# Attention with a selective layer: transposes in banks of the scores, and up to three small tasks per opening

## The chip, the cores and the metric

The kernel runs on one core of one Trainium2 chip. The metric is the time on the device in microseconds (us), the median of several runs. The engines are named as the profile names them: PE is TensorE (matmuls and transposes), PEld its weight loads, DVE is VectorE, ACT is ScalarE, POOL is GpSimd, SP is SyncE, which issues transfers.

## What is computed

Attention over 8 batches, 12 heads, 448 tokens and a head size of 64, in fp32; queries and keys are normalised before. The result, heads side by side, is the input x (448 tokens of 768 numbers per batch) of a layer that only 128 tokens of each batch pass through: those with the highest score.

```python
def rmsnorm(x, g):
    rms = np.sqrt(np.mean(x * x, axis=-1, keepdims=True) + 1e-06)
    return x / rms * g
q_n, k_n = (rmsnorm(q, g_q), rmsnorm(k, g_k))
scores = scale * np.matmul(q_n, k_n.transpose(0, 1, 3, 2))
scores = scores - np.max(scores, axis=-1, keepdims=True)
attn = np.exp(scores)
attn = attn / (np.sum(attn, axis=-1, keepdims=True) + 1e-09)
out = np.matmul(attn, v)
# ... heads side by side: x is (B, S, H * D)
scores = np.einsum('bsd,d->bs', x, w_gate)
out = x.copy()
for b in range(B):
    top_idx = np.argpartition(-scores[b], capacity)[:capacity]
    xe = x[b, top_idx]
    h = np.maximum(xe @ w1, 0.0)
    ye = h @ w2
    g = 1.0 / (1.0 + np.exp(-scores[b, top_idx]))
    out[b, top_idx] = x[b, top_idx] + g[:, None] * ye
```

## The kernel before

Four heads make a group; there are 24 groups, three to a batch. A group has 7 units of 64 keys, so 168 units in all. A round q of the main loop takes four units: scores and values in turn, two units at a time, and then openings, in which small tasks and pieces of the layers of an earlier batch are put between.

The kernel divides eight banks of PSUM so: four in a ring for the scores (two for each unit), two for the values, one called aux and one called moe.

```python
ps_sc = ctx.enter_context(tc.tile_pool(name="ps_sc", bufs=4, space=PSUM))
ps_av = ctx.enter_context(tc.tile_pool(name="ps_av", bufs=2, space=PSUM))
ps_aux = ctx.enter_context(tc.tile_pool(name="ps_aux", bufs=1, space=PSUM))
ps_moe = ctx.enter_context(tc.tile_pool(name="ps_moe", bufs=1, space=PSUM))

def aux(shape, name):
    if PER * now[0] >= units:              # attention is over
        return ps_sc.tile(shape, F32, tag="sc", name=name)
    if spare[0]:                           # no piece of the layers here
        return ps_moe.tile(shape, F32, tag="moe", name=name)
    return ps_aux.tile(shape, F32, tag="aux", name=name)
```

When the last unit of a group has its values, four tasks follow. `sum_keys` multiplies the sums of the probabilities with a small matrix (den_ps, line 360), and ACT copies the result to SBUF (den). `invert_sums` transposes it (denT_ps, line 375), and DVE takes the reciprocal (rden). `to_tokens` transposes the result of a pair of heads (x_ps, line 389; two pairs in a group, c = 0 and 1), and DVE multiplies it with rden into x (line 391). `last_tokens` does pair 1 and lets the gate scores follow.

```python
def to_tokens(n, c):
    # ...
    t = xTs.pop((n, c))
    ps = aux([128, NJ, 128], "x_ps")
    for j in range(NJ):
        nc.tensor.transpose(out=ps[:CP, j, :], in_=t[:, j, :], identity=ident)
    # ... DVE: x = ps * rden

def finish(n, q):
    # ...
    task((q, 1), sum_keys, n)
    task((q, 2), invert_sums, n)
    task((q + 1, 0), to_tokens, n, 0)
    task((q + 1, 1), last_tokens, n)
```

An opening does one task, the first that is due. When a batch's x is whole, `score_rows` transposes the gate scores (row_ps, line 444), ACT copies them to SBUF (score_rows), DVE ranks the tokens, and the selected rows go through DRAM and come back as xe. `mixture` is a generator of pieces: two halves of the selected rows' transposes (line 523), the first product (line 542), the second (line 561); its banks are moe's.

```python
for a in range(2):
    ps = bank()                            # ps_moe, or ps_sc after the attention
    for i in range(half):
        nc.tensor.transpose(...)           # 3 x 128 columns of xe
    nc.scalar.copy(out=xeT[...], in_=ps[...])
    # ...
    yield
```

The main loop, where `ready` holds the round from which a batch's layers may start:

```python
def opening(q, place):
    now[:] = q, place
    for i, (when, fn) in enumerate(tasks[:2]):
        if when <= (q, place):
            tasks.pop(i)
            fn()
            return

while done < B or tasks:
    now[:] = q, 0
    k = PER * q
    for half in range(HALVES):
        for u in (k + 2 * half, k + 2 * half + 1):
            if u < units:
                scores(u)                  # two banks of the ring, 8 matmuls, 2 exps on ACT
        run_values(k + 2 * half - 1, q)    # 8 matmuls a unit; DVE sums the probabilities
    opening(q, 0)
    for half in range(HALVES):
        run((k + 2 * half, k + 2 * half + 1))   # loads, squares, scaling, gate ...
        some = piece(q)                    # a piece of the layers, if there is one
        spare[0] = not some and half == 0
        if some or half == 0 or len(tasks) > 2:
            opening(q, half + 1)
        spare[0] = False
        run(())
    q += 1
```

Instructions stand on each engine in the order of the program.

Of the kernel before, what the change touches and what calls it, by code (L numbers as in the profile page):

```python
# [10 lines left out]
F32 = mybir.dt.float32  # L11
# [57 lines left out]
def fast(  # L69
# [23 lines left out]
    B, NP, _, S = loads.src["qT"].shape  # L93
    CP = 112
    NJ = S // CP
# [24 lines left out]
    ps_sc = ctx.enter_context(tc.tile_pool(name="ps_sc", bufs=4, space=PSUM))  # L120
# [4 lines left out]
    spare = [False]  # L125

    def aux(shape, name):

        if PER * now[0] >= units:
            return ps_sc.tile(shape, F32, tag="sc", name=name)  # L130
        if spare[0]:
            return ps_moe.tile(shape, F32, tag="moe", name=name)
        return ps_aux.tile(shape, F32, tag="aux", name=name)

# [23 lines left out]
    ps = ps_moe.tile([128, 512], F32, tag="moe", name="warm_ps")  # L158
# [121 lines left out]
    def scores(u):  # L280
        n, i = divmod(u, NI)
        scs = [ps_sc.tile([128, 512], F32, tag="sc", name="sc") for _ in range(2)]
        for c in range(2):
            for k0 in (0, 32):
                for hh in range(2):
                    r = slice(D * hh, D * (hh + 1))
                    o = D * c + k0
                    nc.tensor.matmul(  # L288
                        out=scs[hh][o : o + 32, 0:S],
                        lhsT=get("kT", n)[r, c, D * i + k0 : D * i + k0 + 32],  # L290
                        rhs=get("qT", n)[r, c, :],
                        start=True,
                        stop=True,
                    )
        p = p_pool.tile([128, 2, S], F32, name="p")
        for hh in range(2):
            nc.scalar.activation(  # L297
                out=p[:, hh],
                in_=scs[hh][:, 0:S],
                func=AF.Exp,  # L300
                scale=rinvs[n, 1][:, hh, i : i + 1],
            )
        probs[u] = p
# [78 lines left out]
    def to_tokens(n, c):  # L382
        b = n // NG
        if b not in xs:
            xs[b] = x_pool.tile([CP, NJ, DX], F32, name="x")
        t = xTs.pop((n, c))
        ps = aux([128, NJ, 128], "x_ps")
        for j in range(NJ):
            nc.tensor.transpose(out=ps[:CP, j, :], in_=t[:, j, :], identity=ident)  # L389
        col = (n % NG * 2 + c) * 128  # L390
        nc.vector.tensor_tensor(  # L391
            out=xs[b][:, :, col : col + 128].rearrange("p j (h d) -> p j h d", d=D),
            in0=ps[:CP].rearrange("p j (h d) -> p j h d", d=D),
            in1=rdens[n][:, :, :, c, None].to_broadcast([CP, NJ, 2, D]),
            op=OP.mult,
        )
# [109 lines left out]
    def mixture(b):  # L506

        n = CAP
        xe = xes.pop(b)
        xeT = moe_pool.tile([128, NDC, 128], F32, name="xeT")  # L510

        def bank():

            if PER * now[0] >= units:
                return ps_sc.tile([128, 512], F32, tag="sc", name="sc")
            return ps_moe.tile([128, 512], F32, tag="moe", name="moe_ps")

        half = NDC // 2
        for a in range(2):
            ps = bank()  # L520
            for i in range(half):
                dc = half * a + i
                nc.tensor.transpose(
                    out=ps[:, 128 * i : 128 * i + n],
                    in_=xe[:n, 128 * dc : 128 * (dc + 1)],
                    identity=ident[:n, :n],
                )
            nc.scalar.copy(
                out=xeT[:, half * a : half * (a + 1), :n],
                in_=ps[:, : half * 128].rearrange("p (i t) -> p i t", t=128)[:, :, :n],  # L530
            )
            if a == 1:
                row = moe_pool.tile([128, 1], I32, name="row", bufs=2)
                nc.vector.tensor_copy(out=row[:n], in_=xe[:n, DM + 1 : DM + 2])
            yield

        hT = moe_pool.tile([128, NFC, 128], F32, name="hT")
        for f0 in range(0, NFC, 4):
            ps = bank()
            for i in range(4):  # L540
                for dc in range(NDC):
                    nc.tensor.matmul(  # L542
                        out=ps[:, 128 * i : 128 * i + n],
                        lhsT=w1[:, dc, 128 * (f0 + i) : 128 * (f0 + i + 1)],
                        rhs=xeT[:, dc, :n],
                        start=(dc == 0),
                        stop=(dc == NDC - 1),
                    )
                if i == 1:
                    yield  # L550
            nc.scalar.activation(
                out=hT[:, f0 : f0 + 4, :n],
                in_=ps.rearrange("p (i t) -> p i t", t=128)[:, :, :n],
                func=AF.Relu,
            )
            yield
        for a in range(2):
            cols = slice(DM // 2 * a, DM // 2 * (a + 1))
            ps = bank()
            for fc in range(NFC):  # L560
                nc.tensor.matmul(  # L561
                    out=ps[:n, : DM // 2],
                    lhsT=hT[:, fc, :n],
                    rhs=w2[:, fc, cols],
                    start=(fc == 0),
                    stop=(fc == NFC - 1),
                )
                if fc == NFC // 2 - 1:
                    yield
            nc.vector.scalar_tensor_tensor(  # L570
                out=xe[:n, cols],
                in0=ps[:n, : DM // 2],
                scalar=xe[:n, DM : DM + 1],
                in1=xe[:n, cols],
                op0=OP.mult,
                op1=OP.add,
            )
            if a == 1:
                nc.gpsimd.indirect_dma_start(  # L579
                    out=out.flatten_outer_dims(),  # L580
                    out_offset=bass.IndirectOffsetOnAxis(ap=row[:n, :1], axis=0),
                    in_=xe[:n, 0:DM],
                    in_offset=None,
                )
            yield
# [9 lines left out]
    todo, tasks = {}, []  # L595
# [4 lines left out]
    now = [0, 0]  # L600

    def task(when, fn, *args):
        tasks.append((when, lambda: fn(*args)))

    def opening(q, place):
        now[:] = q, place
        for i, (when, fn) in enumerate(tasks[:2]):
            if when <= (q, place):
                tasks.pop(i)
                fn()  # L610
                return

    def prepare(n, slot):
        sq = {}
# [23 lines left out]
    def finish(n, q):  # L638

        if n == n_groups - 1:  # L640
            for fn, args in ((sum_keys, (n,)), (invert_sums, (n,)), (to_tokens, (n, 0))):
                task((q, 1), fn, *args)
            task((q, 1), last_tokens, n)
            return
        task((q, 1), sum_keys, n)
        task((q, 2), invert_sums, n)
        task((q + 1, 0), to_tokens, n, 0)
        task((q + 1, 1), last_tokens, n)

    def soon():  # L650

        q, place = now
        return PER * q + 2 * place if PER * q < units else -9
# [30 lines left out]
    def run_values(upto, q):  # L684
        ended = False
        while waiting and waiting[0] <= upto:
            u = waiting[0]
            if ended and u % NI == 0:

                return  # L690
            values(waiting.pop(0))
            if u % NI == NI - 1:
                values_out(u // NI)
                finish(u // NI, q)
                ended = True
            add_probs(u)
# [11 lines left out]
    def run(slots):  # L708
        for slot in sorted(x for x in todo if x < 0 or x in slots):
            for fn in todo.pop(slot):  # L710
                fn()
# [14 lines left out]
    moe, ready, done, q = iter(()), {}, 0, 0  # L726
# [6 lines that stand above are left out]
                    scores(u)  # L733
            run_values(k + 2 * half - 1, q)
        opening(q, 0)
        for half in range(HALVES):
            run((k + 2 * half, k + 2 * half + 1))
            some = piece(q)
            spare[0] = not some and half == 0
            if some or half == 0 or len(tasks) > 2:  # L740
                opening(q, half + 1)
            spare[0] = False
            run(())
        q += 1
# [532 lines left out]
```

## Time and profile before

| what | value |
|---|---|
| time, median of 3 runs | 543.69 us (543.24 to 544.44) |
| span of the profiled run | 541.9 us |
| mean granted clock of PE | 0.993 |
| ACT busy | 278.2 us (51%) |
| POOL busy | 242.3 us (45%) |
| transfers | 93.57 MB, mean 173 GB/s |
| first product of the layers (line 542) begins | 126.9 us |
| last product of the layers ends | 531 us |

A line of a group in the profile gives the source line, the engine, the operation, what it writes and reads, the shape and the count; then the busy time in us and the mean duration of one in ns; then the idle time of the engine just ahead of it, and what ended most of it. A line of the timeline gives start and length in us, and the count of the instructions that it merges; in square brackets, the idle time before it and who ended it. PE has two records for each fp32 matmul, so a unit's 8 score matmuls stand there as 16 records and a pair of units as 32. Matmuls that run side by side in parts of the array overlap in the records; their ends are modelled.

### The profile page before, as it was taken

To read this page: it belongs to the slowest core of one execution; us is meant where nothing else is said; L and a number is where in the kernel's file an instruction comes from. 1 tells how busy PE (TensorE), PEld (TensorE's weight loads), DVE (VectorE), ACT (ScalarE), POOL (GpSimd) and SP (SyncE) were. 2 spreads that over 40 slices of the span, in tenths; PEclk is the share of its full clock that TensorE was granted. 3 is DMA by queue.
4 is the path that set the end of the run, shared out by engine and by line. 5 is a ranking of instruction groups with operands and counts; after the bars stand their busy time and mean duration, and the time that the engine had idled before them with its cause. 6 is when DMAs were issued, how large, how long until landed. Compare 5 with 4: busy or idle time off the path is not lost. (4 is left out here: it accounts for less than half of the span.)

```text
span 541.9 us, 16470 instructions
## 1 busy us (share of the span) xinstructions
PE 514.9 (95%) x7116; PEld 288.7 (53%) x7116; DVE 339.8 (63%) x644; ACT 278.2 (51%) x506; POOL 242.3 (45%) x193
## 2 busy tenths in 40 slices
PE   6999899999999999999999999999999999999991
PEld 5534344446644375546644466443664456568770
DVE  3767898888475776659557794668746384343000
ACT  3787786784535754446445745547454344311000
POOL 4876988558624176244634456246732103002000
PEclk9999999999999999999999999999999999999997
DMA  8857879999951496508726486605924031004100
GB/s 308 340 164 245 283 245 340 300 304 306 299 181 36 145 256 209 199 31 249 223 101 206 137 250 215 206 2 161 288 86 137 31 104 60 2 20 141 60 4 33
DMA packets 41605, 93.57 MB, mean 173 GB/s; under 512 B 6454, under 2 KB 24374, under 8 KB 41524
## 3 DMA queue, kind: packets, MB, share of 16 engines
q1 hardware_dynamic: 36772, 85.96, 50.1%
q0 software_dynamic: 4608, 6.47, 3.6%
q8 instruction: 58, 0.95, 0.7%
q14 instruction: 23, 0.19, 0.1%
q10 hardware_dynamic: 144, 0.00, 0.0%
HBM read 74.93 MB, written 25.35 MB: 185 GB/s over the span
## 5 line engine op out<-in xcount | busy, mean ns | idle before, releaser
L297 ACT ACTIVATE p<-sc,rinv 128x448 f32<-128x448 f32 x336 | 186.3, 639 | 109.7 <-PE sc L288 88.7
L314 PE MATMUL av<-p,v 64*32 64x448 f32 x2688 | 159.2, 537 | 0.0
L288 PE MATMUL sc<-qT,kT 64*32 64x448 f32 x2688 | 153.1, 540 | 0.3
L212 POOL TENSOR_TENSOR rinv<-ss,neg_half 128x14 f32<-128x14 f32 x48 | 138.6, 2888 | 4.0
L331 DVE TENSOR_TENSOR sum<-sum,p 128x896 f32<-128x896 f32 x113 | 122.5, 1084 | 8.9 <-ACT p L297 1.7
L314 PEld LDWEIGHTS av<-p,v 64*32 64x32 f32 x2688 | 58.7, 107 | 78.1 <-issue 72.0
L209 POOL TENSOR_SCALAR ss<-ss 128x14 f32<-128x14 f32 x48 | 22.8, 475 | 160.4 <-DVE ss L208 134.4
L288 PEld LDWEIGHTS sc<-qT,kT 64*32 64x32 f32 x2688 | 49.4, 106 | 70.0 <-issue 47.4
L542 PE MATMUL moe_ps<-xeT,w 128*128 128x128 f32 x576 | 69.4, 277 | 0.8 <-issue 0.8
L208 DVE TENSOR_REDUCE ss<-sq 128x14 f32<-128x896 f32 x48 | 51.4, 1077 | 29.7 <-ACT sq L202 26.1
L542 PEld LDWEIGHTS moe_ps<-xeT,w 128*128 128x128 f32 x576 | 66.3, 192 | 5.1 <-issue 5.1
L391 DVE TENSOR_TENSOR x<-x_ps,rden 112x512 f32<-112x512 f32 x48 | 32.9, 689 | 55.1 <-PE x_ps L389 50.8
L561 PE MATMUL moe_ps<-w,hT 128*128 128x384 f32 x176 | 61.2, 491 | 0.0
L485 POOL DMA_INDIRECT selected<-x,rank x32 | 36.2, 1131 | 35.0 <-DVE x L477 26.2
L202 ACT ACTIVATE sq<-tok 128x896 f32<-128x896 f32 x48 | 45.9, 962 | 6.8 <-DMA tok<-in_tok_dram 6.7
L579 POOL DMA_INDIRECT out_dram<-xe,row x8 | 10.8, 1354 | 79.8 <-DVE rden L377 47.7
L561 PEld LDWEIGHTS moe_ps<-w,hT 128*128 128x128 f32 x176 | 31.7, 190 | 21.8 <-issue 2.9
L415 DVE SCALAR_TENSOR_TENSOR prod<-x,wg 112x256 f32<-112x256 f32 x96 | 40.9, 426 | 3.0
L226 POOL DMA_DIRECT2D rows<-rinv x44 | 29.1, 662 | 6.6 <-POOL rinv L212 6.5
L389 PEld LDWEIGHTS x_ps<-ident,xT 128*112 128x112 f32 x192 | 21.0, 133 | 18.9 <-issue 12.7
L389 PE MATMUL x_ps<-ident,xT 128*112 128x128 f32 x192 | 29.1, 278 | 1.4 <-DVE x L391 1.4
L570 DVE SCALAR_TENSOR_TENSOR xe<-sc,xe 128x384 f32<-128x384 f32 x5 | 3.1, 618 | 41.0 <-PE sc L561 41.0
(66 smaller groups left out, 339.7 us busy)
## 6 DMA issues: line engine op xcount, KB each, us to landing
tok<-in_tok_dram SPq DMA_DIRECT2D x48, 448.0 KB
qT<-in_qT_dram SPq DMA_DIRECT2D x24, 448.0 KB
kT<-in_kT_dram SPq DMA_DIRECT2D x24, 448.0 KB
v<-in_vp_dram SPq DMA_DIRECT2D x24, 448.0 KB
out_dram<-x SPq DMA_DIRECT2D x8, 1344.0 KB
bc<-rows SPq DMA_DIRECT2D x44, 224.0 KB
xe<-selected SPq DMA_DIRECT2D x8, 385.0 KB
w<-in_moe_w_dram SPq DMA_DIRECT2D x6, 512.0 KB
```

The costliest lines, as they stand in the source:

```text
L202: nc.scalar.activation(out=sq, in_=t, func=AF.Square, scale=scale)
L208: nc.vector.tensor_reduce(out=ss, in_=sq, axis=AX.X, op=OP.add)
L212: nc.gpsimd.tensor_tensor(out=rinv.rearrange(flat), in0=ss.rearrange(flat), in1=neg_half.to_broadcast([128, 2 * NI]), op=OP.pow,)
L288: nc.tensor.matmul(out=scs[hh][o : o + 32, 0:S], lhsT=get("kT", n)[r, c, D * i + k0 : D * i + k0 + 32], rhs=get("qT", n)[r, c, :], start=True,
L297: nc.scalar.activation(out=p[:, hh], in_=scs[hh][:, 0:S], func=AF.Exp, scale=rinvs[n, 1][:, hh, i : i + 1],)
L314: nc.tensor.matmul(out=avs[n][c][o : o + 32, 0:S], lhsT=get("v", n)[r, hh, i, d0 : d0 + 32], rhs=probs[u][r, hh], start=(i == 0), stop=(i ...
L331: nc.vector.tensor_tensor(out=sums[n], in0=probs[u - 1] if i == 1 else sums[n], in1=probs[u], op=OP.add)
L389: nc.tensor.transpose(out=ps[:CP, j, :], in_=t[:, j, :], identity=ident)
L415: nc.vector.scalar_tensor_tensor(out=prod, in0=xs[b][:, j, cols], scalar=1.0, in1=wg[:, cols], op0=OP.mult, op1=OP.mult, accum_out=gates[b ...
L485: w = nc.gpsimd.indirect_dma_start(out=t[:, :], out_offset=bass.IndirectOffsetOnAxis(ap=rank[:, j : j + 1], axis=0), in_=x[:, j, :], in_of ...
L542: nc.tensor.matmul(out=ps[:, 128 * i : 128 * i + n], lhsT=w1[:, dc, 128 * (f0 + i) : 128 * (f0 + i + 1)], rhs=xeT[:, dc, :n], start=(dc == 0),
L561: nc.tensor.matmul(out=ps[:n, : DM // 2], lhsT=hT[:, fc, :n], rhs=w2[:, fc, cols], start=(fc == 0), stop=(fc == NFC - 1),)
```

## The change

It does four things. The transposes of pair 1 (c = 1) take a bank of the scores' ring instead of aux. So does the second half of the selected rows' transposes, instead of moe. As long as no layers are ready, an opening does up to three tasks, the inversion and both pairs are due together at the beginning of the next round, and the transposed sums take the moe bank, which nothing else needs yet. In that stage the rule of the spare bank no longer applies to other tasks. The aim is that PE need not wait for the one aux bank and the one moe bank to be read before it goes on.

```diff
@@ -128,7 +128,7 @@
 
         if PER * now[0] >= units:
             return ps_sc.tile(shape, F32, tag="sc", name=name)
-        if spare[0]:
+        if spare[0] or name == "denT_ps" and before_layers(now[0]):
             return ps_moe.tile(shape, F32, tag="moe", name=name)
         return ps_aux.tile(shape, F32, tag="aux", name=name)
 
@@ -384,7 +384,8 @@
         if b not in xs:
             xs[b] = x_pool.tile([CP, NJ, DX], F32, name="x")
         t = xTs.pop((n, c))
-        ps = aux([128, NJ, 128], "x_ps")
+        shape = [128, NJ, 128]
+        ps = ps_sc.tile(shape, F32, tag="sc", name="x_ps") if c else aux(shape, "x_ps")
         for j in range(NJ):
             nc.tensor.transpose(out=ps[:CP, j, :], in_=t[:, j, :], identity=ident)
         col = (n % NG * 2 + c) * 128
@@ -517,7 +518,8 @@
 
         half = NDC // 2
         for a in range(2):
-            ps = bank()
+
+            ps = ps_sc.tile([128, 512], F32, tag="sc", name="xeT_ps") if a else bank()
             for i in range(half):
                 dc = half * a + i
                 nc.tensor.transpose(
@@ -604,11 +606,12 @@
 
     def opening(q, place):
         now[:] = q, place
-        for i, (when, fn) in enumerate(tasks[:2]):
-            if when <= (q, place):
-                tasks.pop(i)
-                fn()
-                return
+        for _ in range(3 if before_layers(q) else 1):
+            for i, (when, fn) in enumerate(tasks[:2]):
+                if when <= (q, place):
+                    tasks.pop(i)
+                    fn()
+                    break
 
     def prepare(n, slot):
         sq = {}
@@ -643,9 +646,18 @@
             task((q, 1), last_tokens, n)
             return
         task((q, 1), sum_keys, n)
+        if before_layers(q):
+
+            task((q + 1, 0), invert_sums, n)
+            task((q + 1, 0), to_tokens, n, 0)
+            task((q + 1, 0), last_tokens, n)
+            return
         task((q, 2), invert_sums, n)
         task((q + 1, 0), to_tokens, n, 0)
         task((q + 1, 1), last_tokens, n)
+
+    def before_layers(q):
+        return done == 0 and ready.get(0, q + 1) > q
 
     def soon():
 
@@ -736,7 +748,7 @@
         for half in range(HALVES):
             run((k + 2 * half, k + 2 * half + 1))
             some = piece(q)
-            spare[0] = not some and half == 0
+            spare[0] = not some and half == 0 and not before_layers(q)
             if some or half == 0 or len(tasks) > 2:
                 opening(q, half + 1)
             spare[0] = False
```

## The prediction

> **What bounds the kernel now.** I read the page's busy times first, then the groups, then the waits of TensorE (PE), then the timelines of PE and VectorE (DVE) around the transposes.
>
> ```profile
> PE 514.9 (95%) x7116; PEld 288.7 (53%) x7116; DVE 339.8 (63%) x644; ACT 278.2 (51%) x506; POOL 242.3 (45%) x193
> L314 PE MATMUL av<-p,v 64*32 64x448 f32 x2688 | 159.2, 537 | 0.0
> L288 PE MATMUL sc<-qT,kT 64*32 64x448 f32 x2688 | 153.1, 540 | 0.3
> ```
>
> PE works almost without a break from 5 us to 531 us, and the idle time in front of its two largest groups is nil, so only waits of PE itself are worth anything. Its waits, longest first, leaving out the start:
>
> ```profile
> PE moe_ps L523 <- ACT xeT L528: 2.1, 3, 1.2
> PE den_ps L360 <- DVE x L391: 2.1, 5, 0.5
> PE denT_ps L375 <- ACT den L368: 1.8, 3, 0.9
> PE denT_ps L375 <- DVE prod L415: 1.4, 1, 1.4
> PE x_ps L389 <- DVE x L391: 1.4, 3, 0.5
> ```
>
> Columns: total us, times, longest. All five are waits for a bank, or for the den copy in SBUF, and sum to 8.8 us: 1.6% of 543.7. That is the ceiling of what the change can take away.
>
> Matmul spans overlap, so I also measure from start to start. In the timeline a block of 32 score or value matmuls (two units) takes 1.50 us (38.24 to 39.74), so a unit 0.75, and the four blocks of a round 6.2 us. Four rounds are 2 to 3 us longer (near 89, 138, 391 and 450 us) where PE's weight loads show only "issue"; I take these as random and keep them.
>
> DVE is at 63% on average, but the table by windows shows 9.69, 9.48 and 9.50 busy us of 10 from 60 to 90 us, the stage before the layers, where the new task rule acts.
>
> **What the Trainium skill says.** "Perfetto Trace Analysis", [...]"Optimizing Tensor Performance", Matmuls: independent groups should rotate through different banks, so that evacuation overlaps the next group. That is the idea of the change; the 8.8 us agree that single banks cost something. "PSUM — Partial Sum Buffer", section "Engine vs sequencer instructions": VectorE and ScalarE queues are strict FIFO and matmuls start in program order. The trace agrees, and this decides my sign: a score matmul that waits for a bank holds everything behind it, and a bank's reader stands behind all earlier work of its engine.
>
> **The change part by part.** The order of instructions in the changed program has as many matmuls in the fast part as before; nothing is computed less.
>
> *Removed.* (a) Before the layers denT moves behind the next round: its four waits go, 1.8 + 1.4 = 3.2 us. (b) Pair 1 no longer waits for the aux bank: 1.4 us. (c) Of the five waits of den for DVE x, three come after pair 1 and go (0.46 + 0.45 + 0.46 = 1.4); two (44 and 103 us) stay, as pair 0 is still in aux. (d) The second half of the selected rows does not wait for the first copy (2.1 us), but denT follows it and needs the den copy, which ACT does behind that same copy: at 311.83 for 0.36 us, so denT could start at about 312.25, against 312.38 now. Worth 0.15 us each, 0.5 in all. (e) Some six fewer switches between small and full array tiles, about 0.1 us each (a block's last gap is 0.09 us longer): 0.6. Sum: 3.2 + 1.4 + 1.4 + 0.5 + 0.6 = 7.1 us.
>
> *Added: pair 1 in the ring of the scores.* The ring has four banks, a unit takes two. Pair 1 takes one; the next unit takes two, and the second bank of the unit after that is pair 1's. Its matmuls start 0.78 us after the first unit's and then wait for DVE to read pair 1. The trace has what that costs:
>
> ```profile
> 51.66 0.60 PE L389 MATMUL x_ps<-ident,xT 128*112 128x128 f32 x4
> 52.19 1.73 PE L288 MATMUL sc<-qT,kT 64*32 64x448 f32 x32
> 50.76 2.29 DVE L331 TENSOR_TENSOR sum<-sum,p 128x896 f32<-128x896 f32 x2
> 52.96 0.25 DVE L377 RECIPROCAL rden<-denT_ps 112x16 f32<-112x16 f32 x1
> 53.32 0.69 DVE L391 TENSOR_TENSOR x<-x_ps,rden 112x512 f32<-112x512 f32 x1
> ```
>
> DVE reads pair 0 here 1.1 us after the scores have begun, because of its sums. With three tasks per opening the order is denT, pair 0, pair 1, scores, and on DVE rden, x, x. Let T be the end of the values. PE reaches the second unit at T + 0.22 + 0.87 + 0.09 + 0.78 = T + 1.96. DVE, if idle, gets pair 0 at T + 0.86 (data lands 0.31 us after the last start) and ends pair 1 near T + 2.25: a wait of 0.3 us. Where DVE is late by its sums, more. Carrying DVE's queue forward op by op with the traced steps (ss 1.0, sum 1.07 to 1.15, gate product 0.47, scaling 1.07, x 0.65):
> - the openings now at 51.7, 67.8, 84.0 and 110.7 us have scores right behind: DVE ends pair 1 near 54.1, 68.9, 86.6 and 112.8 in the changed order, and PE reaches the second unit near 52.6, 68.6, 84.5 and 112.3; waits 1.5, 0.3, 2.1 and 0.5 = 4.4 us
> - at 42.9 and 101.9 us the den matmuls stand between; scores are free, but den's wait for pair 0 grows from 0.35 to 0.5: 0.3 us.
>
> *Added: spare bank not used before the layers.* den now follows row_ps in aux and needs the score_rows copy: near 75 us 0.8 us (copy ends at 76.19 in the trace, and the order of the two is the same); near 118 us row_ps moves a round earlier and the copy stands behind two xT copies (0.98 us), 1.6 us. Together 2.4.
>
> *Added: with layers.* Pair 1 right before scores, no product of the layers between:
>
> ```profile
> 302.96 0.69 DVE L391 TENSOR_TENSOR x<-x_ps,rden 112x512 f32<-112x512 f32 x1 [2.48 <-PE x_ps L389]
> 303.56 1.07 DVE L208 TENSOR_REDUCE ss<-sq 128x14 f32<-128x896 f32 x1
> 304.56 0.68 DVE L391 TENSOR_TENSOR x<-x_ps,rden 112x512 f32<-112x512 f32 x1
> ```
>
> The ss stands between the two reads also in the changed order. Pair 1 is read until 305.24 and the second unit would begin at 303.29 + 0.78 = 304.07: 1.2 us. In the same way 0.6 at 243 us, and 0.15 each at 283, 364 and 386: 2.2 us. Where a product of the layers follows (2.7 us), nothing.
>
> *Added: selected rows in the ring.* Their copy stands on ACT behind a Square of 0.96 us in four of six places:
>
> ```profile
> 181.27 0.50 ACT L528 COPY xeT<-moe_ps 128x384 f32<-128x384 f32 x1
> 181.64 0.98 ACT L202 ACTIVATE sq<-tok 128x896 f32<-128x896 f32 x1
> 182.65 0.48 ACT L528 COPY xeT<-moe_ps 128x384 f32<-128x384 f32 x1
> ```
>
> The copy ends near 183.1 to 183.3 while PE, freed of two waits of 0.46, is at the second unit at 182.28 + 0.78 = 183.06: 0.2 us. Also near 121, 312 and 372: 0.8 us.
>
> Sum added: 4.4 + 0.3 + 2.4 + 2.2 + 0.8 = 10.1 us. Net 10.1 − 7.1 = +3.0. I take off 1.7: a wait lets DVE and ACT catch up, so neighbouring waits overlap, and the wait of 2.1 at 84 us stands just ahead of the issue gap at 89, which may fill in the meantime. That leaves +1.3: 543.7 + 1.3 = **545.0 us**.
>
> **The rivals.**
> - *The waits simply go.* If DVE or ACT keep up better than I carried forward, the scores do not wait, and some 6 us are won: 537 to 538. For it: the 8.8 us are real, and PE's other time does not change. Against it: DVE's 95% from 60 to 90 us, and reads of pair 1 that ended up to 2.3 us after the second unit's start (88.08 against 85.76).
> - *DVE becomes the bound before the layers.* Then every bank wait counts in full and the issue gaps stay: nothing comes off the sum and further waits join: net +4 to +6, 548 to 550.
> - *Transfers.* Stores of x and loads move by about a round, and DMA is at 1.0 busy share around 80 to 90 and 100 to 140 us; issue gaps may shift by 2 us either way. This widens the range only.
>
> **Range and chances.** My sum says +3, the discount +1.3, the rival that all goes well −6, the other +6. Range 538.5 to 550. Two per cent is 10.9 us: faster by that is over the 8.8 us ceiling, 0.01; slower needs 554.6, far beyond my full sum, 0.03; within 0.96. Which side of 543.7 it falls on I hold open, about three in five for slower.
>
> **What would show it.** Right: PE's waits list denT and x_ps no more, and score matmuls of L288 appear in it with DVE x (and ACT xeT) as releasers, some 5 to 10 times, 0.2 to 2 us each; den waits for score_rows near 76 and 119 us. The first layers' product starts no earlier than its 126.9 us of now. Wrong: the L288 group still has idle time under 2 us, and the stage before the layers ends earlier; then DVE read pair 1 in time, and the step that carries its queue forward failed. A change that sits in the long rounds near 89, 138, 391 and 450 us would be none of my steps.

## The result, and the profile after

The changed kernel takes 546.29 us (median; 545.62 to 547.38) against 543.87 us for the kernel before in the same rounds: ratio 1.0047, 95% interval 1.0026 to 1.0068. It is a little slower. Spans of the profiled runs: 541.9 us before, 545.6 after.

The page of the changed kernel: the lines that answer to those of the prediction (busy us, share, instructions; groups with busy us, mean ns, idle time ahead) and the clock of PE in 40 slices:

```profile
PE 520.4 (95%) x7116; PEld 298.3 (55%) x7116; DVE 341.4 (63%) x644; ACT 278.2 (51%) x506; POOL 240.5 (44%) x193
L288 PE MATMUL sc<-qT,kT 64*32 64x448 f32 x2688 | 167.0, 544 | 0.9 <-DVE x L392 0.7
L314 PE MATMUL av<-p,v 64*32 64x448 f32 x2688 | 163.6, 537 | 0.0
PEclk9999999998999999999999999999999999999997
```

Its six largest waits of PE, without the start (total us, times, longest):

```profile
PE den_ps L360 <- DVE sum L331: 3.0, 2, 2.3
PE denT_ps L375 <- ACT den L368: 1.4, 2, 0.9
PE denT_ps L375 <- issue: 1.2, 1, 1.2
PE den_ps L360 <- ACT score_rows L449: 0.9, 2, 0.6
PE den_ps L360 <- DVE x L392: 0.7, 2, 0.3
PE sc L288 <- DVE x L392: 0.7, 2, 0.4
```

The waits for a bank at x_ps and at the selected rows are gone, as intended. In their place den waits for something it never waited for, DVE's sums, and slice 10 of the clock is no longer 9. The two lines of busy PE rise with nothing added and with the mean of one hardly changed (544 and 537 ns, against 540 and 537): their records overlap less.

With time counted in each profile from its first score matmul, the changed kernel is 1.2 us late at unit 48, 4.0 us late at unit 72 (175 us on that count) and 3.0 us late at the end. So it loses 4 us before the layers and in their first rounds, and gains 1 us after. How it loses is best seen in DVE's timeline from 53 us on. First the kernel before, behind the read of pair 0 at 53.32 that the prediction shows (start us, length us):

```profile
53.92 1.08 DVE L208 TENSOR_REDUCE ss<-sq 128x14 f32<-128x896 f32 x1
54.92 2.21 DVE L331 TENSOR_TENSOR sum<-sum,p 128x896 f32<-128x896 f32 x2
58.30 0.69 DVE L391 TENSOR_TENSOR x<-x_ps,rden 112x512 f32<-112x512 f32 x1 [1.17 <-PE x_ps L389]
```

The same stretch of DVE's timeline in the changed kernel:

```profile
53.73 1.29 DVE L392 TENSOR_TENSOR x<-x_ps,rden 112x512 f32<-112x512 f32 x2
55.05 0.42 DVE L416 SCALAR_TENSOR_TENSOR prod<-x,wg 112x256 f32<-112x256 f32 x1
...
56.80 1.08 DVE L208 TENSOR_REDUCE ss<-sq 128x14 f32<-128x896 f32 x1
57.80 2.67 DVE L331 TENSOR_TENSOR sum<-sum,p 128x896 f32<-128x896 f32 x2
```

Both pairs and the four gate products (55.05 to 56.8) now stand ahead of the sums, which end at 60.47 instead of 57.13. PE's timeline of the changed kernel shows what follows from that, here and once more near 122 us:

```profile
53.03 1.69 PE L288 MATMUL sc<-qT,kT 64*32 64x448 f32 x18
55.07 0.60 PE L288 MATMUL sc<-qT,kT 64*32 64x448 f32 x7 [0.35 <-DVE x L392]
...
60.53 0.59 PE L360 MATMUL den_ps<-sum,pick_pair 128*32 128x224 f32 x8 [0.72 <-DVE sum L331]
...
122.05 0.58 PE L360 MATMUL den_ps<-sum,pick_pair 128*32 128x224 f32 x8 [2.32 <-DVE sum L331]
...
123.77 2.83 PE L288 MATMUL sc<-qT,kT 64*32 64x448 f32 x32
```

The second unit of the block at 53.03 should start 0.78 us on, at 53.81. Two of its sixteen records do start early, and the others begin at 55.07: 1.26 us late, of which the profile shows only 0.35 as idle, because those two fill the rest. Then den waits for the sums. At 122 us the same happens with 2.32 us. There four products and the spreading of the gate stand ahead of the three sums (first fence), while in the kernel before the sums come first and pair 1 after them (second fence):

```profile
114.99 0.42 DVE L416 SCALAR_TENSOR_TENSOR prod<-x,wg 112x256 f32<-112x256 f32 x1
117.05 0.39 DVE L432 COPY spread<-gate 112x448 f32<-112x448 f32 x1
118.50 3.40 DVE L331 TENSOR_TENSOR sum<-sum,p 128x896 f32<-128x896 f32 x3
```

```profile
113.56 3.40 DVE L331 TENSOR_TENSOR sum<-sum,p 128x896 f32<-128x896 f32 x3
117.30 0.69 DVE L391 TENSOR_TENSOR x<-x_ps,rden 112x512 f32<-112x512 f32 x1 [0.33 <-PE x_ps L389]
```

The pair of units behind it has 2.83 us of matmuls instead of 1.7, and the table by windows (us; PE busy; granted clock; DMA share; GB/s) says why:

```profile
120.00:122.00 2.00, 0.00 (x0) 1.00 1.02 396
122.00:123.00 1.00, 0.95 (x11) 0.83 1.03 406
123.00:125.00 2.00, 2.00 (x20) 0.50 1.04 401
125.00:126.00 1.00, 1.00 (x16) 0.50 1.01 399
```

After the idle time the clock was halved for 3.413 us. The kernel before shows no halved clock between 9 and 534 us. By estimate it costs half of 3.4, 1.7 us.

### The profile page after: what moved, and what is told of

It is laid out like the page before. It is cut to its first block, busy times and chain, and to the rows that moved or that the text cites. A ratio compares the mean times of both kernels' runs of the same rounds, so it can differ in the third digit from the quotient of the medians.

```text
span 545.6 us, 16474 instructions
## 1 busy us (share of the span) xinstructions
PE 520.4 (95%) x7116; PEld 298.3 (55%) x7116; DVE 341.4 (63%) x644; ACT 278.2 (51%) x506; POOL 240.5 (44%) x193
## 5 line engine op out<-in xcount | busy, mean ns | idle before, releaser
L288 PE MATMUL sc<-qT,kT 64*32 64x448 f32 x2688 | 167.0, 544 | 0.9 <-DVE x L392 0.7
L314 PE MATMUL av<-p,v 64*32 64x448 f32 x2688 | 163.6, 537 | 0.0
L314 PEld LDWEIGHTS av<-p,v 64*32 64x32 f32 x2688 | 63.7, 107 | 70.6 <-issue 58.6
L288 PEld LDWEIGHTS sc<-qT,kT 64*32 64x32 f32 x2688 | 54.8, 106 | 76.3 <-issue 49.1
L209 POOL TENSOR_SCALAR ss<-ss 128x14 f32<-128x14 f32 x48 | 20.1, 419 | 165.0 <-DVE ss L208 149.1
L341 ACT COPY xT<-av 128x448 f32<-128x448 f32 x48 | 23.4, 548 | 11.2 <-PE av L314 8.5
L331 DVE TENSOR_TENSOR sum<-p 128x896 f32<-128x896 f32 x24 | 25.8, 1073 | 4.6 <-ACT p L297 4.6
```

The lines of the kernel that those rows point to most:

```text
L288: nc.tensor.matmul(out=scs[hh][o : o + 32, 0:S], lhsT=get("kT", n)[r, c, D * i + k0 : D * i + k0 + 32], rhs=get("qT", n)[r, c, :], start=True,
L314: nc.tensor.matmul(out=avs[n][c][o : o + 32, 0:S], lhsT=get("v", n)[r, hh, i, d0 : d0 + 32], rhs=probs[u][r, hh], start=(i == 0), stop=(i ...
L331: nc.vector.tensor_tensor(out=sums[n], in0=probs[u - 1] if i == 1 else sums[n], in1=probs[u], op=OP.add)
```

## Experiments

Three theories: **ring** (a score bank held by pair 1 costs the time), **DVE** (the three-task rule puts work ahead of the sums that den waits for; banks only decide where the wait shows), and **clock** (part of the loss is the half clock after a long wait). Each ratio is against the kernel before on the same chip, whose median was 534.53, 542.45 and 542.74 us in the three batches; microseconds are compared inside a batch only.

### The two stages apart (batch 1)

First, the ring only with layers; the stage before them as it was:

```diff
-ps = ps_sc.tile(...) if c else aux(shape, "x_ps")
+ps = ps_sc.tile(...) if c and not before_layers(now[0]) else aux(shape, "x_ps")
 # opening: range(1); finish: no early tasks; spare as before; denT in aux
```

> Ring banks for pair 1 and the selected rows only once layers run; the stage before the layers as in the kernel before. Theory (the loss of about 2.4 us arises before the layers, the ring pays a little with layers): 1 us faster than before, 542.0 to 543.5; TensorE (PE) has no den or moe_ps wait for DVE x or for the first copy after 117 us, and score waits of about 1.2 us at 303 us and 0.3 us at 243 us. Rival (the ring costs wherever it is used): 545 or more.

Measured 533.15 us, 0.9976 (0.9965 to 0.9987): faster. Second, the reverse, ring and new order only before the layers:

```diff
+ps = ps_sc.tile(...) if c and before_layers(now[0]) else aux(shape, "x_ps")
-ps = ps_sc.tile([128, 512], ...) if a else bank()
+ps = bank()
```

> The new order before the layers with pair 1 in the ring there; with layers the banks of the kernel before. Theory: the loss is all here, 546 to 548 (slower than before by 2.5 to 4 us), with den waiting over 2 us near 122 us and the clock at one half for 3.4 us after it. Rival (ring costs wherever it is used): at most 545.

Measured 539.47 us, 1.0085 (1.0070 to 1.0101): 4.9 us slower, more than the 2.5 to 4 expected. The loss lies in the stage before the layers alone; with the layers the ring pays. The sum of the two, +0.6%, is near the whole change's 0.47%.

### Spare bank, and a later gate (batch 1)

The spare rule given back, so that den need not wait for pair 0 or score_rows:

```diff
-spare[0] = not some and half == 0 and not before_layers(q)
+spare[0] = not some and half == 0
```

> The changed kernel, but small tasks may use the spare moe bank before the layers as they did. Theory: the two waits of den for DVE x (0.35 us each) and the one of 0.62 us for the score_rows copy near 77 us go, the one of 2.3 us near 122 us stays, as it waits for the sums on DVE: 1.3 us less than the changed kernel, 545. Rival (bank of den is what holds it at 122 us too): that wait and the half clock go as well, 3 to 5 us less, 541 to 543.

Measured 537.51 us, 1.0058 (1.0041 to 1.0075): no gain to be seen, neither against the changed kernel's 1.0047 on another chip nor against the 1.0061 of the two runs above. The waits for x and score_rows near 77 us went, but scores now wait 2.6 us for x, and den still 3.0 us for sums. This profile has a den wait of 2.3 us at 120.57 and no halved clock.

One gate, that of batch 1's last group, a round later, so that its products and the spreading do not stand ahead of the sums at 118 us:

```diff
+late = 1 if b == 1 and g == NG - 1 else 0
-s = soon()
+s = soon() + PER * late
```

> The changed kernel, but the gate scores and ranking of batch 1 come one round later, so that DVE has the sums of group 6 ahead of them. Theory (den at 122 us waits for DVE's queue, and the idle time makes the clock fall): that wait of 2.3 us shrinks under 0.7 us, the clock stays at 1.0 there, 3 to 4.5 us less than the changed kernel: 542 to 543.5. Rival (clock and long round at 124 to 134 us have nothing to do with the wait): at most 2 us less, and the half clock is still there.

Measured 535.34 us, 1.0013 (1.0002 to 1.0024). The wait of 2.3 us and the half clock are gone. In PE's timeline of this kernel den follows at once:

```profile
119.03 0.55 PE L525 MATMUL moe_ps<-ident,xe 128*128 128x128 f32 x3
119.67 0.59 PE L360 MATMUL den_ps<-sum,pick_pair 128*32 128x224 f32 x8
121.51 0.43 PE L375 MATMUL denT_ps<-ident,den 128*112 128x128 f32 x2 [0.78 <-ACT den L368]
```

Against the changed kernel's 1.0047 on another chip that is some 1.8 us less, against the sum of the first two runs here, 1.0061, some 2.6; expected were 3 to 4.5. The wait of 0.78 for the den copy takes back part of the 4 us that wait and clock together cost.

### Which banks? (batch 2)

The changed kernel again, as the yardstick of this chip:

> The changed kernel, unaltered, timed beside the three others. Theory: 1.004 to 1.006 of the kernel before. Den waits for the sums on DVE for about 2.3 us near 120 us; whether the clock falls to one half after it varies from run to run. Rival (the loss belongs to the first chip, where long issue gaps stood): at most 1.002.

545.54 us, 1.0055 (1.0034 to 1.0076). Then, before the layers, pair 1 in moe and denT in the ring, so that the scores wait only for the small reciprocal:

```diff
+if name == "denT_ps" and before_layers(now[0]):
+    return ps_sc.tile(shape, F32, tag="sc", name=name)
 # pair 1 before the layers: ps_moe.tile(shape, F32, tag="moe", name="x_ps")
```

> The changed kernel, but before the layers pair 1 takes the moe bank and the transposed sums take the ring's, whose reader on DVE (the reciprocal) stands 1.4 us ahead of the reading of pair 1. Theory (score matmuls wait in the ring for DVE to read pair 1): the long rounds near 52 and 86 us, 2.1 us too long each in the changed kernel, shrink to under 0.8 us too long, total 2.5 to 3.5 us less than the changed kernel, 0.998 to 1.001 of before. Rival (those rounds are long for another reason, weights or transfers): within 1 us of the changed kernel.

Measured 546.60 us, 1.0075 (1.0050 to 1.0100): a miss, and the one that decides. DVE's and PE's timelines of this kernel (its lines are numbered two higher):

```profile
57.31 2.66 DVE L333 TENSOR_TENSOR sum<-sum,p 128x896 f32<-128x896 f32 x2
60.03 0.59 PE L362 MATMUL den_ps<-sum,pick_pair 128*32 128x224 f32 x8 [2.01 <-DVE sum L333]
```

The scores of that round no longer wait. Den waits 2.01 us instead of 0.72, and the round is again 2.1 us too long. The same debt to DVE shows at the next place; ring falls as the cause there. At the other place that was expected to shrink, near 86 us, no den follows directly, and there the ring did hold the scores: the second unit is 0.44 us late in this kernel and 1.88 us in the changed one beside it. The halved clock appears twice, for 3.413 us each, behind den waits of 2.0 and 2.6 us.

With layers, the ring only where no spare bank is there (the stage before them again as it was):

```diff
+ps = ps_sc.tile(...) if c and not before_layers(now[0]) and not spare[0] else aux(shape, "x_ps")
```

> Ring banks only once layers run, and pair 1 there only where no spare moe bank is at hand, so that the opening near 300 us goes back to moe. Theory: the 1.3 us that the round near 300 us is too long goes, all else as in the run with the ring only with layers: 0.995 of before (0.9940 to 0.9965). Rival (what is spared there turns up as a wait further on): 0.997 to 0.998.

Measured 539.83 us, 0.9948 (0.9927 to 0.9968): **faster than both kernels** (against the changed one on the same chip 0.9895, 0.9876 to 0.9915, worked out from the scatter of 7 and 6 runs). With layers, where scores follow pair 1 directly, ring still was the right theory: the first experiment (first fence) waits inside the pair of units, this one (second fence) does not.

```profile
297.59 1.69 PE L288 MATMUL sc<-qT,kT 64*32 64x448 f32 x18
299.60 0.60 PE L288 MATMUL sc<-qT,kT 64*32 64x448 f32 x7 [0.32 <-DVE x L392]
```

```profile
299.05 1.08 PE L390 MATMUL x_ps<-ident,xT 128*112 128x128 f32 x8
300.06 1.74 PE L288 MATMUL sc<-qT,kT 64*32 64x448 f32 x32
```

The first experiment with the selected rows left in moe:

```diff
-ps = ps_sc.tile([128, 512], F32, tag="sc", name="xeT_ps") if a else bank()
+ps = bank()
```

> Ring only once layers run and only for pair 1; the selected rows' second half stays in moe. Theory (pair 1 in the ring frees aux and is what pays; the selected rows' ring bank moves its wait from the transposes to denT and to the scores): pair 1's waits for aux go, the waits of moe_ps for the first copy come back: 0.997 to 0.999, as the run with both. Rival (the selected rows pay): 0.9995 or more.

Measured 542.32 us, 1.0000 (0.9984 to 1.0017): a miss. Its waits of PE show what the second bank of the selected rows is worth; none of this kind is left in the kernel that beats both:

```profile
PE moe_ps L525 <- ACT xeT L530: 3.0, 5, 1.2
```

Its median is 2.5 us above the best kernel's. It also has the 1.3 us round at 300 us, which the best kernel lacks; the other 1.2 us, by this subtraction, fall to the selected rows. So by this reckoning it was their bank that paid in the first experiment; pair 1 in the ring, with layers, paid nothing by itself (1.0000).

### Less or later work for DVE (batch 3)

In the changed kernel the gate products of batches 0 and 1 cover 16 of 256 columns. This leaves out most of the gate scores, and other rows are selected; everything else is done.

```diff
+w = 16 if n < 2 * NG else GH * D
-prod = moe_pool.tile([CP, GH * D], F32, name="prod")
+prod = moe_pool.tile([CP, GH * D], F32, name="prod")[:, 0:w]
```

> The changed kernel with the gate products of batches 0 and 1 over 16 of the 256 columns of a group (the rest of these products is left out, so other rows are selected there). It takes some 1.3 us of DVE work per group out of the stage before the layers, and nothing of TensorE's. Theory (DVE's queue is what limits that stage, and the waits for the ring and for den are only the places where it shows): the waits at 52, 86 and 120 us fall under 1 us each, 4 to 6 us less than the changed kernel, 0.994 to 0.998 of the kernel before. Rival (the banks limit, whatever DVE has to do): within 1.5 us of the changed kernel, 1.0025 or more.

Measured 543.38 us, 1.0009 (0.9993 to 1.0025). As a control, the same cut in the kernel before:

> The same cut of the gate products in the kernel before, as a control. Theory: the kernel before had less to gain from DVE, only its wait of denT behind a gate product (1.4 us) and part of the others: 1 to 2.5 us less, 0.9955 to 0.998. Rival (DVE limits both orders alike): as much less as in the changed kernel, 0.992 or below.

Measured 542.51 us, 0.9995 (0.9976 to 1.0013). Less DVE work takes some 2 to 2.5 us off the changed order (from 1.0047 to 1.0055) and 0.2 us, which can't be told from nothing, off the old one; 4 to 6 and 1 to 2.5 us were expected. The wait for sums is gone, and one that the sums had hidden comes up:

```profile
PE den_ps L360 <- ACT score_rows L451: 2.3, 3, 1.4
```

Next, nothing left out: in the changed kernel the gate of all groups of batches 0 and 1 a round later (`late = 1 if n < 2 * NG else 0`, otherwise as in the later gate above).

> The changed kernel with the gate scores of all groups of batches 0 and 1, and what hangs on them, one round later; no work is left out. Theory (it is the order in DVE's queue, gate products ahead of the sums that den needs): den no longer waits for the sums near 60 and 120 us, no half clock near 122 us, ring waits smaller; 2 to 4 us less than the changed kernel, 0.998 to 1.002. Rival (only the amount of work on DVE counts, not its order): within 1 us of the changed kernel.

Measured 543.02 us, 1.0000 (0.9983 to 1.0017): some 2.6 to 3.0 us less than the changed kernel, from moving DVE's work alone, as much as leaving most of the products out gave (543.02 against 543.38 us on the same chip). Den still waits 2.4 us for sums (the longest 1.8), and no halved clock follows.

Last, an attempt to beat the best kernel: there, before the layers, denT also moves a round on, in moe, with pair 1 an opening after it.

```diff
-for _ in range(1):
+for _ in range(2 if before_layers(q) and place == 0 else 1):
 # finish: invert_sums and pair 0 at (q + 1, 0), last_tokens at (q + 1, 1);
 # denT in moe before the layers; batch 1's last gate a round later
```

> Best version so far (ring only with layers and where no spare bank is at hand) with one part of the change before the layers: the transposed sums a round later, in the moe bank, but pair 1 one opening after pair 0 as before, in aux or moe, and the gate of batch 1 a round later. Theory: the four waits of denT (3.2 us) go and little comes back, since nothing of the ring waits for DVE: 1.5 to 3 us less than that version's 0.9948, so 0.990 to 0.993. Rival (DVE limits the stage, what is saved in one wait is paid in the next): 0.994 to 0.997.

Measured 541.47 us, 0.9968 (0.9952 to 0.9984): no better than 0.9948. Its timelines of DVE and PE show the wait that took the place of denT's:

```profile
81.88 4.60 DVE L331 TENSOR_TENSOR sum<-sum,p 128x896 f32<-128x896 f32 x4
86.40 0.25 DVE L377 RECIPROCAL rden<-denT_ps 112x16 f32<-112x16 f32 x1
86.70 0.65 PE L390 MATMUL x_ps<-ident,xT 128*112 128x128 f32 x4 [2.13 <-DVE rden L377]
```

The reciprocal stands behind four sums, and pair 0 behind the reciprocal.

## Why the prediction was right in time, and where its steps failed

The predicted 545.0 us is 1.3 us under the measured 546.29, and its lean to slower held. The mechanism, a bank's reader behind DVE's queue, was right. The terms were not all so.

- **Removed, (a) to (c).** The waits of x_ps and most of denT's before the layers went, as said. Two waits of den for x stay, 0.35 us each (predicted 0.5). No run measures (e), the switches.
- **(d), selected rows.** Where denT follows, 0.50 and 0.93 us of waiting for the den copy remain, as carried forward. But five waits in the kernel that leaves the selected rows in moe, and its 1.2 us against the best one, say that 0.5 was too small.
- **Pair 1 in the ring before the layers, 4.4 us.** Measured from start to start, the second unit was 1.26, 0.40, 0.64 and 0.24 us late at the four places (predicted 1.5, 0.3, 2.1 and 0.5), together 2.5 us. The small figure at the third place is a matter of that profile, in which PE had just stood 1.19 us at denT ("issue") and so gave DVE time. In the repeat of the changed kernel PE did not stand there, and the wait was 1.88 us, with which the sum is 3.8:

```profile
84.86 1.69 PE L288 MATMUL sc<-qT,kT 64*32 64x448 f32 x18
87.52 0.60 PE L288 MATMUL sc<-qT,kT 64*32 64x448 f32 x7 [0.97 <-DVE x L392]
```

So DVE's queue was carried forward well here. What the term misses is the creditor: with pair 1 out of the ring (the kernel with denT in it) the round at 52 was 2.1 us too long all the same.

- **Den behind aux, 2.4 us.** Near 77 us 0.62 against 0.8. Near 119 us 2.32 against 1.6, and released by the sums, not by score_rows: this step failed. It followed ACT's queue there and not DVE's, where pair 1, four products and the spreading of the gate stand ahead of three sums. With the products cut, the predicted wait for score_rows did come up, 1.4 us. That is the rival "DVE becomes the bound before the layers", which I had set against the prediction as an alternative; it was part of the truth.
- **With layers, 2.2 us.** The second unit was 1.22, 0.57, 0.16 and 0.16 us late near 307, 247, 287 and 369 us (predicted 1.2, 0.6, 0.15 and 0.15): right. The stage as a whole gains about 1 us from unit 72 on; the first experiment gains 0.24%, since what (d) takes away there was larger than predicted.
- **Copies of selected rows behind a Square, 0.8 us.** No score wait stands there in the trace. The term was about nil.
- **The discount of 1.7 us.** As a total not borne out: the sum without it, +3.0, is the trace's delay after the first scores, and the median's is +2.4. Its reason does show at one place: in the repeat the wait of 1.88 us at 84.86 us lengthened the way from unit 36 to unit 40 by 0.2 us only (10.94 against 10.73 us in the kernel before, on another chip), as the long round behind it was shorter. That the total came near is partly luck: what was overstated at the ring and the Square was made up by a term that was missing.
- **The missing term: the clock**, 1.7 us. The first product begins at 136.04: "no earlier than 126.9" holds, but by 9 us; the blocks between 123.8 and 135.6 are 4.9 us too long, 1.7 by the clock and the rest without a named wait. A long round of that sort stood one round on in the kernel before.

Open: what makes the long rounds, in which the engines show only "issue". On the chip of batch 1 they hardly occur, which goes with its 534.53 us for the kernel before. No experiment aimed at them.

## What to carry to other kernels

A second bank paid here only where its reader was not behind other work: ask which engine empties the bank and what is ahead in its queue. Where that engine was 95% busy, changing banks moved the wait on, while putting what PE needs next ahead of what nobody waits for shortened it. Give a ring's bank to a side task where a large product follows, and a spare bank where the ring's own user follows directly.

## What the runs showed of the hardware

A short pause of PE can cost more than its length. Six pauses in five profiles were each followed by 3.413 us at half clock, by estimate some 1.7 us more: 2.3 us in the changed kernel and again in its repeat, 2.2 us with the change only before the layers, 2.0 and 2.6 us with denT in the ring, 2.1 us in the last kernel. Pauses of 1.8 us (all gates later) and of 2.3 us (spare rule given back) were not.

The traces show what parts them. In each of the 14 profiles every change of the clock lies a whole multiple of 3.4133 us after the first one, so each trace can be divided into windows of that length. The window with the pause and the one behind it (us; PE busy; granted clock; DMA share; GB/s), in the changed kernel and then in the spare-rule kernel:

```profile
119.25:122.66 3.41, 1.09 (x14) 1.00 1.02 400
122.66:126.07 3.41, 3.41 (x37) 0.50 1.03 402
```

```profile
119.01:122.42 3.41, 1.85 (x25) 1.00 1.05 408
122.42:125.83 3.41, 3.41 (x81) 1.00 1.03 377
```

The two pauses are equally long, but the second one, from 118.25 to 120.57 us, is cut in two by the boundary at 119.01. Up to 500 us, over all profiles, the clock was halved behind the six windows in which the trace has PE idle for 1.96 us or more, and behind none in which it was idle for 1.84 us or less. So what counts is the idle time inside one window, and a pause of some 2 us could bring the half clock in one execution and not in the next. This is read off the traces and no run was made to test it; near 520 us, where other matmuls run, two windows with 1.95 and 2.01 us idle had no half clock behind them.

The Trainium skill, "TensorE: Matmul & The Clock Gate", section "What's actually happening", gives a free-running window of 3413 ns and half the clock after at least one idle window. The length agrees to the nanosecond; the idle time needed does not, as 1.96 us of the 3.41 sufficed here.
